# Attention and soft mixture of experts on one core: new TensorE order, V asked for two iterations before its cast, and on-chip homes for all experts' weights

## The chip, the cores and the metric

The kernel runs on one core of a Trainium2 chip. The metric is the device time of one execution in microseconds (us), as the median of several executions. Most numbers about stages come from one profiled execution of each kernel, whose span is 1.5 to 2 us shorter than the time of the same run. The profiled run of the kernel before took 241.13 us, 3.2 us above its median, so differences between its profile and the others may be too large by about that much. A run is called fast when it is within 1.5% of the fastest run of the same kernel, and slow otherwise.

## The reference

Eight batches of eight heads attend causally over 576 tokens and 16 beacon keys. The result, 4608 tokens of 512 values, goes through a soft mixture of eight experts.

```python
scores = scale * np.matmul(q, k_all.transpose(0, 1, 3, 2))   # q, k, v: (8, 8, 576, 64); 16 beacon keys ahead
a = softmax(causal(scores));  x = a @ v_all                   # x: (4608, 512)
logits = x @ phi                                              # 32 slots
slot_input = softmax_over_tokens(logits).T @ x                # (8 experts, 4 slots, 512)
slot_out[e] = np.maximum(slot_input[e] @ w1[e], 0.0) @ w2[e]  # w1: (8, 512, 1024), w2: (8, 1024, 512)
return softmax_over_slots(logits) @ slot_out
```

All inputs are float32: Q and K 18.9 MB, V 9.4 MB, weights 33.55 MB. The output is 9.44 MB. The experts can only start after attention, because `slot_input` needs every token; their weights can come at any time for which there is room.

## The kernel before

Attention runs in 32 iterations, one for each pair of heads. In an iteration the pair's scores are made in four steps (`score`, TensorE, then exp on ScalarE and causal masks on GpSimd), the previous pair is multiplied by V (`attend`), and the next pair's Q and K are transposed (`transp`, TensorE, copied out of PSUM by VectorE). Once in four iterations a batch is complete and its routing pieces (transposes, logits, slot sums) are mixed in.

V of the next batch is requested by SyncE and cast to float16 by GpSimd (even chunks) and VectorE (odd chunks). The weights are requested by GpSimd in pieces of 1 MiB, and the transfer casts them to float16: its queue wrote 16.78 MB for 33.55 MB of float32.

```python
    qkp = ctx.enter_context(tc.tile_pool(name="qkp", bufs=5))     # Q and K pairs
    vfp = ctx.enter_context(tc.tile_pool(name="vfp", bufs=6))     # V chunks
    wh = ctx.enter_context(tc.tile_pool(name="wh", bufs=6))       # weights of six experts
    # ... cut ...
    beacons()
    transp(0)
    for n in range(NP + 1):
        b, g = divmod(n, H // 2)
        # ... cut: flags for the last turn
            score(n, 0)
            for _ in range((0, 2, 3, 2)[n % 4]):
                if work:
                    work.pop(0)()          # routing pieces of the batch before
            score(n, 1)
            transp(n + 1)                  # ends with the copy of the beacon keys on GpSimd
            attend(n - 1, 0)
            score(n, 2)
            attend(n - 1, 1)
            score(n, 3)
            load_pair(n + 5)
            load_v(b + 1, g)               # V chunks 0 and 1, 2, 3, 4 for g = 0, 1, 2, 3
            for c in ((), (0, 1), (2,), (3, 4))[g]:
                cast_v(b + 1, c)           # chunk 4: requested and cast in the same iteration
            if n % 3 != 2 and n >= 3 and wl < 24:
                load_w(wl)                 # one piece of 1 MiB in two of three iterations
                wl += 1
    # ... cut: slot inputs
    layer1(0)
    for e in range(E):
        turn(e)
        if e + 1 < E:
            widen(e + 1)                   # experts 6 and 7 into the buffers of experts 0 and 1
            layer1(e + 1)
        layer2(e)
    # ... cut: output stage
```

The softmax here doesn't subtract the row's maximum and nothing guards it: scores larger than these inputs give would overflow.

## Time and profile before

| | before |
|---|---|
| time, median of 4 runs | 237.95 us (237.39 to 240.46) |
| span of the profiled run (241.13 us) | 239.2 us |
| attention, first to last mask | 12.2 to 171.0 us |
| first matmul of the experts | 181.9 us |
| end of the experts | 210.6 us |
| TensorE busy, share of the span | 74% |
| VectorE, ScalarE, GpSimd | 56%, 56%, 37% |

No engine is busy more than three quarters of the time, so the engines' shares alone name no limit. The prediction below shows how the slices, the list of waits, GpSimd's order of work and the table of stretches are read for it.

### The profile page before, as it was taken

How to read it: one execution, taken by the hardware profiler on the slowest of the kernel's cores; microseconds unless marked ns; L12 is line 12 of the kernel's file. 1: busy time of each engine (PE TensorE's matmuls, PEld its weight loads, DVE VectorE, ACT ScalarE, POOL GpSimd, SP SyncE). 2: the span in 40 equal slices, each digit the busy share in tenths (PEclk: the TensorE clock that was granted, in tenths of full speed). 3: DMA queues.
4: the chain of work that ended last, by engine and by line, in shares of the span. 5: the costliest groups of instructions: out<-in, count | busy, mean ns of one | idle time of the engine just before them, and what ended most of it. 6: DMA issues, size and time to landing. Idle time of an engine off the chain costs nothing.

```text
span 239.2 us, 7827 instructions
## 1 busy us (share of the span) xinstructions
PE 176.9 (74%) x3384; PEld 122.3 (51%) x3384; DVE 134.3 (56%) x315; ACT 133.8 (56%) x195; POOL 88.7 (37%) x165
## 2 busy tenths in 40 slices
PE   0689577987986898997798879799867874578400
PEld 0567455765675776765566666676654221123100
DVE  1591873675777467876576847566654231159600
ACT  2176473677777387886767738487721342149500
POOL 2091625354552644634636165434552700000000
PEclk9999795899999599999979979899995578559955
DMA  6999999999999998999999989564689999919995
GB/s 210 220 328 229 257 256 235 268 201 250 303 271 240 204 258 247 216 285 247 237 307 267 242 180 266 81 95 84 91 137 206 209 206 210 177 77 417 414 425 249
DMA packets 63714, 55.62 MB, mean 233 GB/s; under 512 B 41920, under 2 KB 50112, under 8 KB 62656
## 3 DMA queue, kind: packets, MB, share of 16 engines
q1 hardware_dynamic: 50880, 38.35, 56.9%
q0 software_dynamic: 12800, 16.78, 41.5%
q8 instruction: 26, 0.43, 0.8%
q14 instruction: 8, 0.07, 0.1%
HBM read 62.46 MB, written 9.44 MB: 301 GB/s over the span
## 4 chain that ended last, share of the span: by engine, by line
PE 33%; DMA 27%; ACT 13%; POOL 7%; DVE 5%; SPq 5%; issue 3%; DVEq 0%; ACTq 0%; POOLq 0%
DMA vf<-in_v_dram 17%; ACT ex L209 10%; DMA w2h<-in_moe_w_dram 8%; PE sc L203 8%; PE av L230 6%; PE tr L188 5%; PE tr L257 4%; PE fp L448 3%; SPq L103 2%; ACT osb L450 2%; POOL ex L211 2%; DVE xT L262 2%; PE tr L272 2%; SPq L88 2%; DMA kf<-in_k_dram 2%
## 5 line engine op out<-in xcount | busy, mean ns | idle before, releaser
L209 ACT ACTIVATE ex<-sc 128x1024 f16<-128x1024 f32 (+3 forms) x128 | 107.0, 869 | 59.8 <-PE sc L203 59.5
L203 PE MATMUL sc<-qT,kT 64*128 64x128 bf16 (+5 forms) x576 | 49.8, 269 | 18.5 <-POOL kT L193 8.7
L211 POOL TENSOR_SCALAR_AFFINE_SELECT ex<-ex 128x1024 f16<-128x1024 f16 x32 | 35.0, 1093 | 44.7 <-ACT ex L209 44.6
L230 PE MATMUL av<-vh,ex 128*128 128x65 f16 (+2 forms) x960 | 47.7, 206 | 0.7 <-issue 0.5
L230 PEld LDWEIGHTS <-ex 128*128 128x128 f16 (+2 forms) x960 | 40.2, 113 | 10.2 <-issue 8.3
L203 PEld LDWEIGHTS <-kT 64*128 64x128 bf16 (+1 forms) x576 | 21.7, 106 | 30.1 <-issue 15.3
L190 DVE COPY qT<-tr 128x576 bf16<-128x576 bf16 x32 | 24.2, 757 | 21.3 <-PE tr L188 21.3
L238 DVE TENSOR_TENSOR xb<-av,r 128x320 f16<-128x320 f32 x64 | 31.5, 491 | 2.2
L244 POOL CAST vh<-vf 128x512 f16<-128x512 f32 (+1 forms) x24 | 15.0, 629 | 28.0 <-DMA vf<-in_v_dram 28.0
L190 DVE COPY kT<-tr 128x576 bf16<-128x576 bf16 x32 | 23.9, 748 | 1.0 <-PE tr L188 0.9
L262 DVE COPY xT<-tr 128x1024 f16<-128x1024 f16 x16 | 10.7, 688 | 15.4 <-PE tr L257 15.4
L188 PE MATMUL tr<-idb,kf 64*64 64x64 bf16 x576 | 17.1, 206 | 2.2 <-issue 1.4
L188 PE MATMUL tr<-idb,qf 64*64 64x64 bf16 x576 | 17.1, 208 | 0.0
L188 PEld LDWEIGHTS <-qf 64*64 64x64 bf16 x576 | 13.5, 120 | 6.8 <-issue 6.4
L409 DVE CAST hs<-sc 128x512 f16<-128x512 f32 x8 | 5.5, 691 | 19.2 <-ACT hs L408 19.2
L188 PEld LDWEIGHTS <-kf 64*64 64x64 bf16 x576 | 14.8, 121 | 3.0 <-issue 2.8
L257 PE MATMUL tr<-idh,xb 128*128 128x128 f16 (+1 forms) x160 | 14.2, 247 | 2.3 <-issue 1.2
L217 POOL TENSOR_SCALAR_AFFINE_SELECT ex<-ex 80x160 f16<-80x160 f16 x32 | 10.6, 331 | 13.4 <-ACT ex L209 13.3
L237 DVE RECIPROCAL r<-av 128x5 f32<-128x5 f32 x64 | 12.0, 187 | 5.8 <-PE av L230 5.3
L450 ACT ACTIVATE osb<-fp,rc 128x512 f32<-128x512 f32 x18 | 11.8, 686 | 4.9 <-PE fp L448 4.4
L120 POOL DMA_DIRECT2D w1h<-in_moe_w_dram x16 | 11.5, 724 | 6.7 <-PE sc L404 6.7
L452 DVE TENSOR_SCALAR osb<-fp,rc 128x512 f32<-128x512 f32 x18 | 12.6, 747 | 1.4 <-PE fp L448 1.1
(58 smaller groups left out, 151.1 us busy)
## 6 DMA issues: line engine op xcount, KB each, us to landing
qf<-in_q_dram SPq DMA_DIRECT2D x32, 288.0 KB, 6.2
kf<-in_k_dram SPq DMA_DIRECT2D x32, 288.0 KB, 6.4
w1h<-in_moe_w_dram POOLq DMA_DIRECT2D x16, 512.0 KB, 8.7
w2h<-in_moe_w_dram POOLq DMA_DIRECT2D x16, 512.0 KB, 8.8
out_dram<-osb SPq DMA_DIRECT2D x8, 1024.0 KB, 8.8
vf<-in_v_dram SPq DMA_DIRECT2D x24, 256.0 KB, 7.5
vf<-in_v_dram SPq DMA_DIRECT2D x8, 224.0 KB, 7.2
vf<-in_v_dram SPq DMA_DIRECT2D x8, 160.0 KB, 7.5
```

The lines of the kernel that those rows point to most:

```text
L188: nc.tensor.transpose(tp[po:po + 64, j, :], hi, idb[po:po + 64, po:po + 64])
L190: nc.vector.tensor_copy(out=dst[:, Nb:Nb + S].rearrange("p (s j) -> p s j", j=J), in_=tp[:, :, :].rearrange("p j s -> p s j"))
L203: nc.tensor.matmul(sc[0:kn, a, col:col + un], kT[n % 3][64 * a:64 * a + 64, P * c:P * c + kn], qT[n % 3][64 * a:64 * a + 64, u0:u0 + un], ...
L209: nc.scalar.activation(ex[n][:, :, o:o + w], sc[:, :, 0:w], AF.Exp, scale=scale)
L211: nc.gpsimd.affine_select(out=ex[n][:, :, 0:512].rearrange("p a (c t) -> p a c t", c=4), in_=ex[n][:, :, 0:512].rearrange("p a (c t) -> p ...
L230: nc.tensor.matmul(avs[a][0:m, i * DD:(i + 1) * DD], ex[n][0:kn, a, o:o + m], vh[b % 2][0:kn, c, h, :], start=(c == 0), stop=(c == i))
L238: nc.vector.tensor_tensor(out=xb[b % 2][:, :, h, :], in0=avv[:, :, 0:D], in1=r5[:, :].unsqueeze(2).broadcast_to([P, NCH, D]), op=AL.mult)
L244: (nc.vector if c % 2 else nc.gpsimd).tensor_copy(out=vh[b % 2][0:kn, c, :, 0:D], in_=vf[(b, c)][0:kn])
L257: nc.tensor.transpose(tp[:, ii, t, 0:m], xb[b % 2][0:m, i, 2 * t:2 * t + 2, :].rearrange("p h d -> p (h d)"), idh[0:m, 0:m])
L262: nc.vector.tensor_copy(out=xT[b][:, :, P * cs[0]:P * cs[0] + 2 * P].rearrange("p t (i u) -> p i t u", i=2), in_=tp[:, :, :, :])
L450: nc.scalar.activation(osb[:, j, :], fp_[:, :], AF.Copy, scale=rc[:, i:i + 1])
L452: nc.vector.tensor_scalar(out=osb[:, j, :], in0=fp_[:, :], scalar1=rc[:, i:i + 1], scalar2=None, op0=AL.mult)
```

## The change

The intent is a steady TensorE: transposes two pairs ahead at the end of each iteration, one routing piece at a time, V cast two iterations after its request, and room on chip for the weights of all eight experts, by using the Q, K and V buffers again once they have been read. The weights are asked for at a set pace, faster from iteration 26.

```diff
-    qkp = ctx.enter_context(tc.tile_pool(name="qkp", bufs=5))
-    vfp = ctx.enter_context(tc.tile_pool(name="vfp", bufs=6))
-    wh = ctx.enter_context(tc.tile_pool(name="wh", bufs=6))
+    NQK, NVF, NWB = 5, 6, 6
+    qs = [const.tile([P, J, D], FP, name=f"qs{i}") for i in range(NQK)]
+    # ... ks, vs, wa, wb likewise
+    homes = [wt[:, 1024 * i:1024 * (i + 1)] for e in range(NWB) for wt in (wa[e], wb[e])
+             for i in range(4)]
+    # ... experts 6 and 7: float16 views of qs, ks in the order in which they come free, then vs
+    def pace(n):                           # in half MiB of float32 weights
+        if n < 26:
+            return 2 * max(0, (n - 2) * 16 // 23)
+        return 32 + 4 * (n - 25)
     for n in range(NP + 1):
+            if n + 2 < NP:
+                beacon_keys(n + 2)
             score(n, 0)
-            for _ in range((0, 2, 3, 2)[n % 4]):
-                if work:
-                    work.pop(0)()
             score(n, 1)
-            transp(n + 1)
+        route()                            # one routing piece
             attend(n - 1, 0)
             score(n, 2)
             attend(n - 1, 1)
+        route()
             score(n, 3)
-                load_pair(n + 5)
-                load_v(b + 1, g)
-                for c in ((), (0, 1), (2,), (3, 4))[g]:
-                    cast_v(b + 1, c)
-                load_w(wl)
+            transp(n + 2)
+            load_pair(n + 2 + NQK)
+        for m in ((0, 1) if n == 0 else (n + 1,)):
+            # ... load_v of part m (batch m // 4 + 1)
+        # ... cast_v of part n - 1: requested two iterations before
+        weights(pace(n))
```

## The prediction

> **What bounds the kernel now.** I read the page's forty slices first, then the list of waits, then GpSimd's order of work around one of those waits, and last a table of stretches for what the transfers do. In the slices the last two rows are the transfer engines' busy share and rate, the first the granted TensorE clock.
>
> ```profile
> PEclk9999795899999599999979979899995578559955
> DMA  6999999999999998999999989564689999919995
> GB/s 210 220 328 229 257 256 235 268 201 250 303 271 240 204 258 247 216 285 247 237 307 267 242 180 266 81 95 84 91 137 206 209 206 210 177 77 417 414 425 249
> ```
>
> A slice is 6 us. Transfers are busy everywhere except slices 25 to 28 (150 to 174 us, the last six or so of the 32 pair iterations), where they move 81 to 95 GB/s, and slice 35 (210 to 216 us). Yet slices 30 to 34 (180 to 210 us) are again full, and they are the experts' weights, which could have moved in the hole. That is one loss. The other is in the waits, whose columns are total us, times, longest:
>
> ```profile
> ACT ex L209 <- PE sc L203: 59.5, 69, 9.1
> ...
> POOL vh L244 <- DMA vf<-in_v_dram: 28.0, 9, 5.0
> ...
> PE sc L203 <- POOL kT L193: 8.7, 4, 3.0
> ```
>
> GpSimd waits nine times, 28.0 us in all, to cast a V chunk. It takes its instructions in order, so what stands behind that cast is late too:
>
> ```profile
> 71.73 0.20 POOL L193 COPY kT<-bkT 128x16 bf16<-128x16 bf16 x1
> 76.29 0.61 POOL L244 CAST vh<-vf 80x512 f16<-80x512 f32 x1 [4.37 <-DMA vf<-in_v_dram]
> 76.86 1.09 POOL L211 TENSOR_SCALAR_AFFINE_SELECT ex<-ex 128x1024 f16<-128x1024 f16 x1
> ```
>
> The columns are start, duration, instruction, and idle time before it. The 80-row chunk is asked for and cast in the same iteration (g = 3), so 4.37 us of transfer time are waited out; the mask of the next pair comes 0.6 us after it. That mask marks each iteration; its 32 instances run from 12.2 us to 171.0 us:
>
> ```profile
> L211 POOL TENSOR_SCALAR_AFFINE_SELECT ex<-ex x32: 1085/1091/1112, 12.2 to 171.0; 128x1024 f16<-128x1024 f16 x32
> ```
>
> (171.0 - 12.2) / 31 = 5.12 us an iteration, while the two last, with no V wait, take 4.78 and 4.80 (161.46, 166.24, 171.04). TensorE is busy 134.4 us of that stretch at a mean clock of 0.91, so about 122 / 31 = 3.9 us an iteration at full clock (an estimate; it takes all busy time to scale with the clock). ScalarE is busy 108.6 us, 3.5 an iteration. Neither engine alone accounts for 5.12.
>
> The transfers are nearer to it than they look. In the table of stretches the last two columns are the transfer share (over 1 when two packets overlap) and the GB/s written on chip:
>
> ```profile
> 8.50:12.50 4.00, 2.69 (x68) 2.27 (x68) 2.06 (x4) 1.36 (x2) 0.46 (x2) 1.00 1.36 207
> 14.50:17.50 3.00, 3.00 (x65) 2.43 (x59) 3.00 (x8) 1.93 (x3) 2.80 (x7) 1.00 1.07 393
> 96.00:122.00 26.00, 22.50 (x517) 17.11 (x512) 18.59 (x43) 18.61 (x26) 13.39 (x25) 0.94 1.15 251
> ...
> 150.00:174.00 24.00, 21.16 (x467) 16.14 (x465) 15.36 (x40) 17.43 (x24) 11.27 (x20) 0.93 0.52 83
> ...
> 194.00:200.00 6.00, 4.32 (x64) 1.53 (x57) 2.08 (x3) 2.46 (x5) 0.00 (x0) 0.99 1.21 209
> ...
> 219.00:231.00 12.00, 4.70 (x17) 1.59 (x14) 6.38 (x10) 5.67 (x9) 0.00 (x0) 0.88 1.01 419
> ```
>
> The first row is V alone: 207 GB/s. The second is Q and K alone: 393. The fifth is weights alone: 209 GB/s of float16 written, so 418 of float32 read. The last is the output: 419. From the sizes in the reference: V with its beacons 9.7 MB / 207 = 46.9 us; Q and K 18.9 MB / 393 = 48.0; weights 33.55 MB / 418 = 80.3; small inputs 1; so 176 us of input, and output 9.44 MB / 419 = 22.5. In all 199 of 239 us. The times add when the queues share the engines: from 96 to 122 us the packet counts (6990 under 512 B, so V; 1102 of Q and K; 2.08 MB of weights written) make 8.7 + 6.5 + 10.0 = 25.1 us of such work in 26 us, 96%. So the input transfers are a floor close under everything else.
>
> [...]V goes in 256 B pieces and the trace has it at 207 GB/s against 393 for Q and K in 2304 B pieces[...]the 78 to 84 us slice, after the wait shown, has a clock of 0.5.[...]
>
> **The change, part by part.**
> 1. V is asked for one iteration earlier and cast one later, two iterations apart (about 9 us; the median V landing is 7.1 us, the longest 10.2). All but the very first casts should find their data. Removed: most of the 28.0 us of GpSimd wait[...]. The first batch's request still has one iteration's lag, so one wait near 24 us stays.
> 2. Beacon keys are copied two iterations ahead at the head of GpSimd's work: the 8.7 us of score matmuls waiting for kT go. Transposes two pairs ahead at the end of an iteration take their copies off the path to the next score; the routing pieces come one per slot instead of two or three together. The instruction counts on TensorE don't change (6,770 rows in both).
> 3. By iteration 25 both kernels have asked for 16 MiB of weights. After that the old one asks for 4 MiB to iteration 31, then 4, and the last 8 only from 183 us, when the buffers of experts 0 and 1 are read. The new one asks for 12 MiB in the same six iterations and the last 4 directly after, into used Q, K and V buffers. Its cost: up to four issues of 0.72 to 0.76 us on GpSimd in iterations 30 and 31, beside 1.4 us of masks: 4.3 us, just an iteration. The hole of 24 us at 83 GB/s written (166 read, 40% of 418) fills: 14 us.
>
> Sum, on the old trace's clock:
> - First mask at 12.2 us, unchanged.
> - To iteration 25: Q and K 0.59 MB / 393 = 1.50, V 0.303 MB / 207 = 1.46, weights 16.8 MB in 23 iterations, 0.73 MB / 418 = 1.75; 4.7 us of transfer, 4.9 at 96%. Some 8 us may be behind at the end (a weight piece or two in flight, V's two iterations), so I take 4.6 us: above the 4.2 to 4.4 that I estimate for TensorE with few gaps. 25 x 4.6 = 115.
> - Six more at 4.4, with TensorE the limit: 26.4. The last mask is at 153.6, against 171.0.
> - From the last mask to the first expert matmul: 10.8 us (171.04 to 181.86), unchanged. So 164.4.
> - Experts: the first five took 181.86 to 195.47, 2.72 each, mostly at half clock; 8 x 2.72 and 1 for the end make 22.8. So 187.2 if all weights are there.
> - Weights all landed: 2.5 + 176 / 0.95 = 188. The last half expert is used within 1 us: 189. The two limits nearly meet; I take 189, against 210.6 in the old trace.
> - From there to the end 28.6 us (210.6 to 239.2), of which 22.5 are the output. Span 217.6; the old span is 1.5 above the median time, so 216 us.
>
> The gain of about 21 us is not the sum of what is removed (28 of GpSimd waits, 8.7 of kT, 14 of hole, and these expert stalls):
>
> ```profile
> 202.39 0.61 PE L404 MATMUL sc<-w1h,siT 128*32 128x512 f16 x2 [2.37 <-DMA w1h<-in_moe_w_dram]
> ...
> 204.94 1.04 PE L404 MATMUL sc<-w1h,siT 128*32 128x512 f16 x6 [1.94 <-DMA w1h<-in_moe_w_dram]
> ```
>
> They overlap, and the transfers' floor stops all of them.
>
> **Rivals.** (a) Transfers stay at 96% or better and the hole goes completely: last weight at 183, experts at full clock, 211 us. For it: stretches of the old trace reach it. Against: start-up, and the expert stage ran at half clock. (b) The faster attention makes the queues collide: V, in small packets beside more weights, comes later than two iterations, the casts wait again, only later, and transfers run at 90%: last weight at 198, about 225 us. For it: landings up to 10.2 us, near the 9.2 us lag. Against: the lookahead of Q and K grows too, and a late weight costs attention nothing. (c) GpSimd or VectorE becomes the bound: four weight issues and the masks in the last iterations, or VectorE's 105 us in the 159 us stretch packed into 141. It would add 3 to 5 us, 220. (d) All weights on chip but nothing gained, because only the order of the same bytes moves: excluded by the hole, which is real idle time.
>
> **Range and chances.** 216.5 us, 210 to 224 from (a) and most of (b). Over 2% faster needs below 232.9; even (b) gives that. Faster 0.96, same 0.03, slower 0.01.
>
> **What would show it.** Last mask near 154 us; GpSimd's wait for V under 8 us, mostly near 24 us; no score wait for kT; no hole before the last mask, transfers full to about 188; the experts with little or no wait for weights; clock 0.9 or more in attention; the output stage unchanged. It is wrong if iterations stay near 5 us with V waits (b), if TensorE alone holds them at 4.8, or if experts 6 and 7 still wait several us for weights.

## The result, and the profile after

The changed kernel takes 228.97 us (median of 4 runs, 227.28 to 230.84) beside 237.95 for the kernel before. The ratio is 0.958, with a 95% interval of 0.947 to 0.969. A ratio here is the mean time of one kernel's fast runs over that of the other's of the same rounds, so it is not quite the ratio of the medians. The kernel is faster, as forecast, but by 9 us and not by 21, and 229 lies outside the range of 210 to 224.

| | before | predicted | after |
|---|---|---|---|
| last mask (us) | 171.0 | 153.6 | 166.6 |
| first matmul of the experts | 181.9 | 164.4 | 177.1 |
| last weight landed | about 210 | 188 | between 193 and 194 |
| end of the experts | 210.6 | 189 | 198.1 |
| span | 239.2 | 217.6 | 226.5 |

The slices of the changed kernel, in the same rows as before (clock, transfer share, GB/s; a slice is now 5.7 us):

```profile
PEclk9999859997999699859997999997999679959955
DMA  6999989999999999999999999969999999139996
GB/s 202 243 295 381 204 236 258 246 286 215 261 312 216 239 207 246 239 214 227 310 250 264 297 225 241 260 107 208 193 209 209 208 207 205 33 158 416 418 422 255
```

The hole of four slices at 81 to 95 GB/s is gone. One slice with a 6 (slice 26, 147 to 153 us, 107 GB/s) is what remains of it, and from slice 27 to 33 the weights' plain stream runs at 193 to 209 GB/s. So the part of the change that was to fill the hole did so.

The waits (total us, times, longest) are where the surprise is:

```profile
POOL vh L270 <- DMA vs<-in_v_dram: 35.6, 13, 7.8
...
DVE vh L270 <- DMA vs<-in_v_dram: 13.2, 4, 6.3
```

GpSimd waited 28.0 us for V before and waits 35.6 now. VectorE waited 4.6 for V and waits 13.2. Together that is 48.8 us where the prediction had "under 8 us" for GpSimd. The waits of score matmuls for GpSimd's copies into kT are gone from the list, as forecast (one of 0.9 us for VectorE's copy stays, as before). The masks run to 166.6 us:

```profile
L237 POOL TENSOR_SCALAR_AFFINE_SELECT ex<-ex x32: 1090/1094/1139, 12.2 to 166.6; 128x1024 f16<-128x1024 f16 x32
```

The mean iteration is (166.6 - 12.2) / 31 = 4.98 us, only a little under the 5.12 of before, although many iterations without a wait now take 4.1. Two masks are 10.4 us apart around 90 to 100 us. First, from SyncE's order of work, a request for V (start, duration, what is asked for), then, from GpSimd's, a cast and the mask behind it (the last column is the idle time before, and what ended it):

```profile
80.92 0.39 SPq L100 DMA_DIRECT2D vs<-in_v_dram  x1
```

```profile
99.40 0.61 POOL L270 CAST vh<-vs 80x512 f16<-80x512 f32 x1 [7.84 <-DMA vs<-in_v_dram]
...
100.58 1.09 POOL L237 TENSOR_SCALAR_AFFINE_SELECT ex<-ex 128x1024 f16<-128x1024 f16 x1 [0.43 <-ACT ex L235]
```

The V chunk asked for at 80.92 us is cast by VectorE at 95.94, 15.0 us later, and GpSimd waits 7.84 us for another chunk, with the mask of the next pair behind it. Beside it were three pieces of weights, asked for by GpSimd at 79.94, 83.84 and 87.40 us in the view of GpSimd's order. At the solo rates of the prediction, three pieces are 3.15 MB / 418 = 7.5 us. SyncE's requests from 74.84 to 80.92 us, four of Q and K and two of V, are 3.0 and 2.5 us. That is an estimate of 13.0 us for what was in front of the chunk or beside it.

The experts run from their first matmul to the end without a wait for weights, in 21.1 us:

```profile
177.05 1.04 PE L449 MATMUL sc<-wa,siT 128*32 128x512 f16 x8
...
198.13 0.75 DVE L477 TENSOR_SCALAR soh<-av,rd 128x512 f16<-128x512 f32 x1 [1.91 <-PE av L467]
```

Before they took 28.8, with 5.4 us of waits for weights in the trace. The output stage takes 28.4 us (28.6 before).

### The profile page after: what moved, and what is told of

The parts are those of the page before. It is cut to its first block, busy times and chain, and to the rows that moved or that the text cites.

```text
span 226.5 us, 7849 instructions
## 1 busy us (share of the span) xinstructions
PE 167.2 (74%) x3384; PEld 118.3 (52%) x3384; DVE 136.5 (60%) x315; ACT 131.0 (58%) x195; POOL 93.2 (41%) x173
## 4 chain that ended last, share of the span: by engine, by line
PE 30%; DMA 26%; ACT 15%; DVE 11%; SPq 6%; issue 4%; POOL 2%; DVEq 0%; ACTq 0%; POOLq 0%
DMA vs<-in_v_dram 22%; ACT ex L235 10%; PE sc L229 7%; PE av L256 7%; PE tr L212 5%; DMA qs<-in_q_dram 3%; PE sc L449 3%; SPq L100 3%; DVE hs L454 2%; PE fp L489 2%; SPq L89 2%; PE tr L283 2%; ACT hs L453 2%; DVE xT L288 2%; DVE xb L264 2%
## 5 line engine op out<-in xcount | busy, mean ns | idle before, releaser
L237 POOL TENSOR_SCALAR_AFFINE_SELECT ex<-ex 128x1024 f16<-128x1024 f16 x32 | 35.1, 1096 | 39.3 <-ACT ex L235 39.3
L229 PE MATMUL sc<-qT,kT 64*128 64x128 bf16 (+5 forms) x576 | 44.6, 263 | 4.3 <-ACT ex L235 2.0
L270 POOL CAST vh<-vs 128x512 f16<-128x512 f32 (+1 forms) x24 | 14.8, 620 | 35.6 <-DMA vs<-in_v_dram 35.6
L229 PEld LDWEIGHTS <-kT 64*128 64x128 bf16 (+1 forms) x576 | 21.2, 103 | 12.5 <-issue 7.2
L263 DVE RECIPROCAL r<-av 128x5 f32<-128x5 f32 x64 | 12.3, 192 | 22.3 <-PE av L256 21.9
L214 DVE COPY kT<-tr 128x576 bf16<-128x576 bf16 x32 | 23.9, 748 | 2.5 <-PE tr L212 2.4
L212 PE MATMUL tr<-idb,ks 64*64 64x64 bf16 x576 | 16.7, 202 | 7.2 <-issue 2.7
L212 PEld LDWEIGHTS <-ks 64*64 64x64 bf16 x576 | 15.5, 116 | 9.3 <-issue 8.7
L212 PE MATMUL tr<-idb,qs 64*64 64x64 bf16 x576 | 16.9, 204 | 2.0 <-DMA qs<-in_q_dram 1.8
L270 DVE CAST vh<-vs 128x512 f16<-128x512 f32 x16 | 10.1, 638 | 13.2 <-DMA vs<-in_v_dram 13.2
L212 PEld LDWEIGHTS <-qs 64*64 64x64 bf16 x576 | 13.0, 117 | 6.2 <-DMA qs<-in_q_dram 2.0
L489 PE MATMUL fp<-soh,eLh 128*128 128x512 f16 x36 | 12.3, 456 | 2.0 <-DVE soh L477 0.8
L302 PE MATMUL tr<-xT,phih 128*128 128x288 f16 x64 | 12.7, 287 | 0.6 <-DVE xT L288 0.3
L283 PEld LDWEIGHTS <-xb 128*128 128x128 f16 (+1 forms) x160 | 10.4, 108 | 3.8 <-issue 3.3
```

Of the source, the lines that this page charges most:

```text
L212: nc.tensor.transpose(tp[po:po + 64, j, :], hi, idb[po:po + 64, po:po + 64])
L214: nc.vector.tensor_copy(out=dst[:, Nb:Nb + S].rearrange("p (s j) -> p s j", j=J), in_=tp[:, :, :].rearrange("p j s -> p s j"))
L229: nc.tensor.matmul(sc[0:kn, a, col:col + un], kT[n % 3][64 * a:64 * a + 64, P * c:P * c + kn], qT[n % 3][64 * a:64 * a + 64, u0:u0 + un], ...
L237: nc.gpsimd.affine_select(out=ex[n][:, :, 0:512].rearrange("p a (c t) -> p a c t", c=4), in_=ex[n][:, :, 0:512].rearrange("p a (c t) -> p ...
L270: (nc.vector if c % 2 else nc.gpsimd).tensor_copy(out=vh[b % 2][0:kn, c, :, 0:D], in_=vs[(NCH * b + c) % NVF][0:kn])
L283: nc.tensor.transpose(tp[:, ii, t, 0:m], xb[b % 2][0:m, i, 2 * t:2 * t + 2, :].rearrange("p h d -> p (h d)"), idh[0:m, 0:m])
```

## The experiments

Theory A: the transfer engines are full, the weights compete there with V, and the waits for V are the symptom. Theory B: V is late because it stands behind Q and K in SyncE's queue with too short a notice. Ratios are to the kernel before in the same rounds. The kernel before and the changed kernel differ by one to two per cent from one set of rounds to the next (the changed kernel had 0.958, 0.968 and 0.952), so kernels are best compared within a set. The waits differ more: the changed kernel's three profiles have 48.8, 67.3 (`after_again`) and 60.5 us (`after_third`, a slow run) of waits for V on GpSimd and VectorE together, and last masks at 166.6, 164.8 and 169.4. Where a profile fell in a slow run this is said, and it is used for waits only.

### First set: what do the weights do to V?

**e2_no_weights.** All weights after attention, in one look.

```diff
     def pace(n):
-        if n < 26: ...
+        return 0
```

> No weights at all are asked for during attention; all 32 MiB come after it. Theory A: the waits for V fall under 12 us in all (mostly the one near 21 to 28 us), iterations take 4.1 to 4.4 us, last mask at 142 to 150. Theory B: the waits stay above 30 us and the last mask after 158. Either way the whole is slower, about 250 us, since 80 us of weights follow attention.

```profile
POOL vh L270 <- DMA vs<-in_v_dram: 7.1, 1, 7.1
...
DVE vh L270 <- DMA vs<-in_v_dram: 5.2, 1, 5.2
```

```profile
L237 POOL TENSOR_SCALAR_AFFINE_SELECT ex<-ex x32: 1090/1096/1098, 12.6 to 145.5; 128x1024 f16<-128x1024 f16 x32
```

Two waits remain, both at the start (before the mask at 26.8 us), and the iterations take 3.99 to 4.38 us from iteration 7 to 30, 4.15 in the mean. The last mask comes at 145.5 us. The whole takes 263.6 us (250 forecast), since 80 us of weights follow. The landings of V, from request to data, in the changed kernel and then here:

```profile
DMA to landing us min/median/max: 3.6/6.8/15.0
```

```profile
DMA to landing us min/median/max: 3.3/4.5/6.6
```

So V's notice is enough without weights beside it, but only just. It isn't the 8.3 us that two iterations would be. Of batches 2 to 6, one chunk is asked for by SyncE and cast by GpSimd at

```profile
70.35 0.38 SPq L100 DMA_DIRECT2D vs<-in_v_dram  x1
```

```profile
77.02 0.61 POOL L270 CAST vh<-vs 128x512 f16<-128x512 f32 x1
```

which is 6.7 us apart, and over all 25 chunks of these batches it is 5.0 to 8.5 us, 6.8 in the mean; each landed at least 0.5 us before its cast. With the weights beside it, half of all landings take 6.8 us or more, and the longest 15.0. (e2 also frees GpSimd of the weights' requests, 0.72 to 0.76 us each; but the landings shorten too, and they don't wait for GpSimd.) The stretch from 30 to 140 us of this run shows what is left for weights (TensorE busy first, clock, transfer share and GB/s last):

```profile
30.00:140.00 110.00, 102.78 (x2555) 80.89 (x2554) 91.38 (x220) 89.54 (x130) 50.53 (x99) 0.98 0.74 193
```

TensorE is busy 102.8 of 110 us here, so 4.15 us is close to the bound of TensorE in this order. Q, K and V need 2.96 us of transfers in each iteration (1.50 + 1.46), which leaves 1.19 us, or 0.50 MB of weights. The change asks for 0.73 MB, 1.75 us. By this estimate it asks for more than fits, and someone must wait. Theory A's forecast is met (the waits are 12.3 us where it had "under 12"), theory B's is not.

**e1_slow_pace.** 12 MiB instead of 16 before iteration 26.

```diff
-            return 2 * max(0, (n - 2) * 16 // 23)
-        return 32 + 4 * (n - 25)
+            return 2 * max(0, (n - 2) * 12 // 23)
+        return 24 + 4 * (n - 25)
```

> Weights asked for more slowly up to iteration 25 (12 MiB in place of 16), the rest later. Theory A (the transfer engines are full, and the weights take their share away from V, so the waits for V are its symptom): GpSimd and VectorE wait for V under 30 us in place of 49, the last mask comes 4 to 8 us earlier than 166.6, but the last weight lands at 190 to 194 as before, so experts 6 and 7 now wait and the whole gains 1 to 4 us. Theory B (V is late because it stands behind Q and K in SyncE's queue and its two iterations are too short a notice): waits for V within 10% of 49 us, last mask within 2 us of 166.6, time within 1%.

The median is 226.19 us, ratio 0.951 (0.942 to 0.961). The waits for V are 17.3 and 3.9 us, the last mask comes at 159.8, 6.8 us earlier, and the experts end at 196.1, only 2 us earlier, because the experts' stage now takes 25.8 us in place of 21.1, with 2.5 us of waits for weights and a mean clock of 0.64 in place of 0.82. Each number is as theory A had it, but the longer stage is only partly a wait for weights. Against the changed kernel the gain is within the noise between sets.

**e3_v_first.** V ahead of Q and K in each iteration.

```diff
-        if n + 2 + NQK < NP:
-            load_pair(n + 2 + NQK)
         for m in ((0, 1) if n == 0 else (n + 1,)):
             ... load_v
+        if n + 2 + NQK < NP:
+            load_pair(n + 2 + NQK)
```

> In each iteration V is asked for before the Q and K pair instead of after it. Theory A: the order in one queue moves about 1.5 us of transfers, waits for V fall by at most a third, time within 1.5% of the changed kernel. Theory B: waits for V fall by half or more (under 25 us), last mask at 158 or earlier, 4 us or more faster than the changed kernel.

The median is 224.80 us, ratio 0.944 (0.935 to 0.953). No run of the changed kernel is in this set; against its 0.952 to 0.968 in others this is 1 to 2.5% faster, about the noise between sets. The waits for V in its profile (a slow run) were 51.3 and 17.1 us. That is no less than in the changed kernel's three profiles, so theory B's forecast of half the waits is refuted, and theory A's of up to a third less isn't met either. Order in the queue by itself doesn't take the waits away.

**e4_v_wide.** V's bytes as rows of 2 KB, wrong (the values land in the wrong places).

```diff
-        nc.sync.dma_start(out=t[p0:p0 + hi - lo], in_=v[b, :, lo:hi, :].rearrange("h p d -> p h d"))
+        nc.sync.dma_start(out=t[p0:p0 + hi - lo].rearrange("p h d -> p (h d)"),
+                          in_=v[b].rearrange("h s d -> (h s d)").rearrange("(p f) -> p f", f=H * D)[lo:hi])
```

> Wrong result on purpose: the same number of V bytes, but read as contiguous rows of 2 KB per partition in place of 256 B pieces, so V should move at nearly 393 GB/s instead of 207: 24 us of transfer work in place of 47. Theory A: waits for V fall under 15 us, last mask at 145 to 155, and the whole is 15 to 22 us faster than the changed kernel (some 207 to 214 us). Theory B, in which the notice and not the amount of transfer counts: it gains too, but less than 8 us.

The median is 218.36 us, ratio 0.915 (0.903 to 0.926): about 10 us faster than the changed kernel (which wasn't in this set), between the two forecasts. The waits were 15.9 and 4.9 us. The last mask came at 156.3 and the experts ended at 188.4 us. The amount of transfer work matters, but 23 us less of it (an estimate, at Q and K's rate) gave less than half of that. What held attention then was not tested; its iterations 7 to 25 still took 4.70 us in the mean, where e2 has 4.14.

### Second set: the parts alone

**e6_before_no_weights.** The kernel before without weights in attention (its three lines around `load_w(wl)` in the loop removed), one look.

> The kernel before, with no weights asked for during attention (they follow, as far as its buffers allow). Told apart from the changed kernel without weights (4.15 us an iteration, one pair of waits for V near 20 us, last mask 145.5), it shows what the order alone is worth when nothing competes. If order and notice matter by themselves: the 80-row chunk, asked for and cast in the same iteration, still makes GpSimd wait in most batches, 10 to 25 us in all, undisturbed iterations stay at 4.7 to 4.8, last mask at 162 to 170. If only the competition of the weights mattered: waits for V under 8 us and last mask under 155.

GpSimd waits 10.3 us for V and VectorE 3.9. That lies in the range of the first forecast by its number only: all but 0.3 us of it comes before 33 us, and not in most batches. The last mask comes at 154.4 us, which fits the second. I had misread the old kernel: its iterations of 4.7 to 4.8 us are followed by one of 3.4 in each batch, so that its undisturbed mean is 4.43 us and not 4.78. Without competition, then, the new order is worth 154.4 - 145.5 = 9 us. With the weights in attention the two orders end only 4.4 us apart (171.0 and 166.6). The notice of V tells what the new loop lost: without weights, the old one has 6.3 to 11.4 us between request and cast for the first four chunks of a batch and 5.0 to 5.4 for the fifth (batches 2 to 6), the new one 5.0 to 8.5 and 6.0 to 6.5. In the program the new notice is an iteration longer. But V stands behind Q and K in SyncE's queue, and these use again the buffers that the new loop's last transposes read in the same iteration, the old loop's in the one before. In the changed kernel's trace SyncE waits 28.1 us in all, in 14 waits, for transposes before it can ask for Q or K; what such waits cost in e2 was not shown.

**e7_homes_only.** The loop of the kernel before, with the new homes and pace.

```diff
-    (loop of the changed kernel)
+    (loop of the kernel before: transp(n + 1), routing in twos and threes, V cast as before;
+     ends with weights(pace(n)))
```

> The old order of the loop with the new homes and the new pace of the weights: the third part of the change alone. Theory A (transfers full, weights compete with V): the last mask does not come earlier than before, 170 to 176; no weights wait at the end; the first matmul of the experts after 181, their end near 204 to 206, and the whole 233 to 236, 1 to 2% faster than before. If the hole were worth its 14 us by itself, it would be 225 or less.

The median is 231.45 us, ratio 0.984 (0.969 to 1.000). The last mask is at 168.9 and the experts end near 200.9 us, somewhat better than forecast. The 14 us of the hole are worth some 4 us by themselves, in an interval that reaches 0.

**e8_order_only** was to be the reverse, the new order with the old weights.

```diff
-    homes += spare
+    homes += homes[0:16]                   # experts 6 and 7 where 0 and 1 were
-        if n < 26: ...                     # pace as in the kernel before
+        return 2 * len([i for i in range(3, n + 1) if i % 3 != 2])
+            weights(8 * (e + 1 + NWB))     # ahead of layer1(e + 1)
```

> The new order, V timing and key copies, with the old weights: 20 MiB during attention, 4 after it, the last 8 into the buffers of experts 0 and 1 when those have been read. Theory A: last mask at 160 to 166, and the experts wait for weights as in the kernel before, ending 28 to 29 us after their first matmul, so 229 to 233 us, 2.5 to 4% faster than before. If the V timing were worth nothing while weights compete: last mask after 168, within 1.5% of before.

It gave a wrong result and 245.61 us: I had put the request for expert 6 ahead of the second layer of expert 0 in program order, so that this layer read expert 6's weights. It tells nothing. **e8b_order_only** puts the request after `layer2(e)`.

> e8 mended: the weights of experts 6 and 7 are asked for after the second layer of experts 0 and 1 has been issued, so they overwrite nothing that is still read. New order and V timing, old weights. Theory A: last mask at 160 to 166 (e8 had 164.4), the experts end 26 to 29 us after their first matmul because the last 8 MiB are asked for only then; 229 to 234 us. With the weights alone at 0.984 of before and the whole change at 0.958, additive parts would give 0.974 here. If the V timing were worth nothing while weights compete: 0.985 or more.

> The changed kernel as it is, once more, to stand beside the others of this call on one chip: 226 to 231 us, 0.95 to 0.965 of before; last mask 163 to 170, waits for V 40 to 70 us.

Both were in one set. e8b has ratio 0.968 (0.957 to 0.979) and the changed kernel 0.968 (0.959 to 0.978). With the old weights the last mask comes at 160.1 us and the first expert matmul at 170.6, but the experts wait and end at 199.0. With the new homes (the profile of that set) the last mask comes at 164.8, the first expert matmul at 175.3, and the experts end at 198.3. So in this set filling the hole gained nothing that can be seen: attention ended 4.7 us later, and the experts' stage (28.4 us without the homes, 23.0 with them) was about as much shorter. The weights of the last iterations explain only a part of the 4.7 us. At iteration 25, where both kernels have asked for 16 MiB, e8b, whose first piece is asked for an iteration sooner, is already 3.2 us ahead (134.7 and 137.8); the six iterations after that take 25.4 and 27.0 us. Whether the parts add isn't settled: e8b's interval holds the 0.974 of its forecast, and 0.968 times e7's 0.984 is 0.953, beside 0.952 to 0.968 for the whole.

### Third set: a better pace and more notice

**c3_deep_slow_vfirst.** Nine V buffers, three iterations of notice, V first, and a slow pace (14 MiB by iteration 28).

```diff
-    NQK, NVF, NWB = 5, 6, 6
+    NQK, NVF, NWB = 5, 9, 6
-        for m in ((0, 1) if n == 0 else (n + 1,)):
+        for m in ((0, 1, 2) if n == 0 else (n + 2,)):   # and ahead of load_pair
-        if n < 26: ...
+        if n < 29:
+            return 2 * max(0, (n - 2) * 14 // 26)
+        return 28 + 4 * (n - 28)
```

> Weights slowed to 12 to 14 MiB up to iteration 28, nine V buffers with V asked for three iterations before its cast, and V ahead of Q and K in the queue. Theory A: waits for V under 20 us, last mask at 148 to 155; the total of transfers is unchanged, so the last weight cannot land before 186 to 190 and the experts wait for it; 217 to 222 us, faster than the changed kernel by 3 to 5%. If transfers are not what limits the whole, the last weight lands before 183 and the time is under 214.

The median is 230.15 us, ratio 0.974 (0.959 to 0.990). The waits for V fell to 8 us as forecast and the last mask came at 156.2 (148 to 155 forecast), but the last weight landed near 199 (186 to 190), and the time was missed by 8 us. The row of GB/s in the slices of c3 shows why (a slice is 5.7 us):

```profile
GB/s 195 240 308 325 211 242 218 286 243 217 325 232 250 298 254 247 292 203 243 320 255 218 313 245 29 115 158 193 203 211 206 209 207 207 131 136 411 426 418 257
```

In slices 24 to 26 (138 to 155 us) the rate is 29, 115 and 158 GB/s: all Q, K and V had been requested and the weights not yet. The old hole had opened again. Attention gained 10 us and the experts, which waited 8 us for weights in all, gave it back.

**c5_ramp11** and **c6_ramp8** were to close it, with 11 and 8 MiB before iteration 24 and three pieces an iteration from there.

```diff
+        if n < 24:
+            return 2 * max(0, (n - 2) * 11 // 21)          # c6: 8
+        return min(48, 22 + 6 * (n - 23)) + 4 * max(0, n - 28)   # c6: 16
```

> As c3 (nine V buffers, three iterations of notice, V ahead of Q and K), but the weights speed up at iteration 24, when the last Q, K and V are asked for, so that the hole of c3 at 130 to 150 us doesn't open; 11 MiB before that. Theory A: last mask 152 to 158, last weight at 180 to 187 and not 198, the whole 216 to 221 us, 4% faster than the changed kernel. If the hole was not what cost c3 its gain: 226 or more.

> As c5 with 8 MiB before iteration 24. Theory A: transfers of Q, K, V and weights then just fit under 4.2 us an iteration, last mask 147 to 153, last weight still 180 to 187 because the total is the same, the experts wait a little for the last weights; 213 to 219 us, the same as c5 or up to 2% faster. If the pace before iteration 24 doesn't matter: last mask as in c5 within 2 us.

Both missed by far: 234.19 us (three of its four runs slow) and 238.34, ratio 0.996 (0.982 to 1.011). The hole did close: no slice is under 157 GB/s until the last weights. In c5 the last V chunks landed up to 23.9 us after their request and GpSimd waited 8.2 and 11.9 us for two of them. In c6 the waits for V were 10.5 us, and its pace (0.40 MB or 0.96 us an iteration before iteration 24) is less than the 1.19 us that e2 leaves. Yet its iterations 7 to 25 took 4.68 us in the mean, with three of 5.3 to 7.1 us between 97 and 116 us, in which TensorE's transposes waited (for what, the trace doesn't say). After that, GpSimd's own requests waited (both profiles are of slow runs):

```profile
163.66 0.53 POOL L138 DMA_DIRECT2D qs<-in_moe_w_dram  x1 [2.00 <-DMA wb<-in_moe_w_dram]
166.22 0.53 POOL L138 DMA_DIRECT2D ks<-in_moe_w_dram  x1 [2.03 <-DMA wb<-in_moe_w_dram]
166.75 1.11 POOL L237 TENSOR_SCALAR_AFFINE_SELECT ex<-ex 128x1024 f16<-128x1024 f16 x1
```

The brackets of the first two lines say that each request for weights waited 2 us until an earlier piece had landed, and the mask at 166.75 us stands behind them. The trace's semaphores show what the wait is: GpSimd's 40 transfers use eight of them in turn, and a request waits until the transfer eight before it has landed. The one at 163.66 us starts 0.3 us after the landing of the piece asked for at 142.39. In the changed kernel's trace the last eleven requests, from 169.50 us on, each start 0.28 to 0.53 us after such a landing. In c6 GpSimd's requests waited 23.5 us in all for earlier pieces, and the masks with them: those at 154.50, 166.75 and 177.00 us are 12.3 and 10.3 us apart.

### Fourth set: one piece at a time

Four kernels in one set of five rounds, with the changed kernel among them. **f1_notice_only** has nine V buffers and three iterations of notice, all else as in the change. **f2_steady_ramp** adds V first and the pace `2 * max(0, (n - 2) * 13 // 23)` up to iteration 25, then `26 + 4 * (n - 25)`. **f3_early_start** is f2 with

```diff
+        if n < 26:
+            return 2 * (n * 14 // 25)
+        return 28 + 4 * (n - 25)
```

> The changed kernel with nine V buffers and V asked for three iterations before its cast in place of two; order in the queue and pace of the weights as they are. If the short notice is what my prediction missed: waits for V 15 to 25 us in place of 49 to 67, last mask 156 to 161, and the whole 1 to 2.5% faster than the changed kernel of this call. If the share that the weights take is what counts and more notice only lengthens the queue: waits for V above 35 us, within 1%.

> Nine V buffers, V ahead of Q and K, 13 MiB of weights before iteration 26 in place of 16, then two pieces of 1 MiB an iteration as in the change. If both V's notice and a weight pace that fits beside 4.2 us iterations are needed: waits for V 10 to 25 us, last mask 153 to 159, last weight 187 to 191 because the transfers' total is what it was, the whole 2 to 3.5% faster than the changed kernel of this call (221 to 225 us). If the last weight is at 195 or later, a hole opened again, as in c3.

> As f2, but the weights start at iteration 2 in place of 4 and reach 14 MiB before iteration 26, so that the stretch from 20 to 40 us, which carried only 83 to 89% of its transfers, is filled. Last weight 2 to 4 us earlier than in f2 (184 to 188) if that stretch was idle for want of requests; the waits for V near 25 us grow by 1 to 3 us; the whole 0 to 1% faster than f2.

> The changed kernel, to stand beside the others of this call: 226 to 231 us.

| | median us | ratio to before | 95% interval |
|---|---|---|---|
| after_third (the change) | 230.39 | 0.952 | 0.945 to 0.959 |
| f1_notice_only | 225.01 | 0.934 | 0.928 to 0.940 |
| f2_steady_ramp | 223.55 | 0.924 | 0.918 to 0.930 |
| f3_early_start | 220.36 | 0.919 | 0.915 to 0.923 |

f1 gains 0.934 / 0.952, 1.8%, with waits for V of 43 us (60.5 in `after_third`; both are slow runs): its times fit one forecast and its waits the other. f2's gain is in its forecast, and in its profile (a slow run) the waits are 13.5 us and the last mask comes at 158.6, but the last weight landed near 192 and not by 191. f3 is 3.4% faster than the change (0.919 / 0.952). Its waits and its masks:

```profile
POOL vh L270 <- DMA vs<-in_v_dram: 6.1, 2, 5.0
...
DVE vh L270 <- DMA vs<-in_v_dram: 4.5, 1, 4.5
```

```profile
L237 POOL TENSOR_SCALAR_AFFINE_SELECT ex<-ex x32: 1084/1090/1197, 12.5 to 157.1; 128x1024 f16<-128x1024 f16 x32
```

10.6 us of waits, last mask at 157.1, experts from 167.6 to 189.1 us, and the span is 217.5. The share of the transfers carried from 20 to 40 us, counted from packets at the solo rates, rose from about 84% in the changed kernel to 96%, and the last weight landed near 186 us, as forecast.

**g1_pace_only** is the changed kernel with the pace of f3 and nothing else, beside **f3_again**, in a last set.

> The changed kernel with the pace of f3 alone (weights from iteration 2, 14 MiB before iteration 26), V with six buffers, two iterations of notice and behind Q and K as in the change. If pace and notice are both needed: waits for V 25 to 45 us, last mask 160 to 166, 224 to 228 us. If the pace was all: waits for V under 15 us and 219 to 222 us, like f3. If the notice was all: 228 to 231 us, like the changed kernel.

> f3 once more, to stand beside g1 on one chip: 219 to 223 us, last mask 155 to 159.

g1 takes 223.17 us, ratio 0.940 (0.928 to 0.952); f3 again 222.85, ratio 0.938 (0.927 to 0.949). They can't be told apart in time. Yet g1's waits for V are:

```profile
POOL vh L270 <- DMA vs<-in_v_dram: 38.3, 17, 6.4
...
DVE vh L270 <- DMA vs<-in_v_dram: 9.1, 6, 5.3
```

47.4 us, as in the change, but in 23 waits of at most 6.4 us, where the changed kernel had 17 of up to 7.8. The last mask is at 160.7 us, against 157 and 161.4 in f3's two profiles (the second is outside its forecast). No forecast of g1 fits whole: mask and waits are nearest to the first, and the time falls between the first two. So the sum of the waits for V is no measure of the time. One reason can be read in the same profiles: GpSimd's idle time before casts and masks together is 74.9 us in the change (35.6 for V, 39.3 for exp), 70.1 in g1 (38.3, 31.8) and 67.6 in f3 (6.1, 61.5). Most of the time in which f3 doesn't wait for V it waits for exp. That a short wait costs little is suggested by this, not shown. The pace alone gives most of what f3 gives. How much the longer notice adds to it stays open within these intervals.

f3 is the fastest correct kernel, and is faster than both the kernel before and the changed one.

## Why the prediction was wrong

The direction was right, and parts 2 and 3 of the mechanism did what they should: the waits for kT went and the hole filled. Part 1 failed, and with it the second term of the sum: "Some 8 us may be behind at the end, so I take 4.6 us". I had worked out 4.9 us of transfers an iteration and then credited 8 us of them to lookahead. The profile has iteration 25 at 137.5 us: (137.5 - 12.2) / 25 = 5.01 us, so 125.3 us in place of 115, more than even 4.9 would give. No such credit is to be seen. Weights that are behind don't lie idle; they share the engines with V, and V is what the next iterations wait for. This rests on e2, where the same loop without weights has 4.15 us an iteration and waits for V only at the start. Part 1's "all but the very first casts should find their data" fell with it: GpSimd waited 35.6 us for V, not under 8.

Part 1 also had its notice wrong. "Two iterations apart (about 9 us)" is 5.0 to 8.5 us even without weights (e2), less than the old loop gave four of five chunks (e6), while half of the change's landings take 6.8 us or more. How much of the 10.3 us each of the two errors cost isn't separated: f1, with one iteration more notice and the same pace, gains 1.8% in its set, and g1, with another pace and the same notice, 1 to 3% against the change in other sets.

By its other steps:

- First mask 12.2 us: measured 12.2.
- Six more iterations at 4.4: 29.1 us in place of 26.4. One wait of 6.15 us for the last batch's V lies in them.
- Last mask to the first expert matmul, 10.8: measured 10.5.
- Experts 22.8: measured 21.1. The first three take 2.67 to 2.78 us each (granted clock 0.60 from 177.05 to 185.2 us) and the later ones 2.24 (0.96 from there to 198.1), so this was too high.
- All weights by 188 us: 193 to 194. 176 us of transfers in 191 us is 92%, not 95%. In the change this wasn't the limit, as its experts didn't wait for weights; in e1 they waited 2.5 us and in c3 8.
- Experts' end to the end of the span, 28.6: measured 28.4.
- The half clock of the old 78 to 84 us slice: TensorE had been idle for 1.8 us (76.2 to 78.0) when the clock fell to 0.5. What lowers it was not shown.
- "The two last, with no V wait, take 4.78 and 4.80" was read rightly but is not the old loop's undisturbed mean, which is 4.43 (e6).

The end of the experts is thus later than the 187.2 of the engines' path by 10.3 + 2.7 - 0.3 - 1.7 = 11.0, with 0.1 lost in rounding: 198.1.

Of the rivals, (b) came closest. It named later V beside more weights, the wait moved and not removed, and landings beyond the lag (15.0 us measured). But it put the damage into the transfers' efficiency, and what bound was the end of attention. I argued against (b) that a late weight costs attention nothing. It was the wrong question: an early weight costs attention its V.

f3's first profile, of the fastest of its six runs, comes near the predicted path: last mask 157.1 (predicted 153.6), first expert matmul 167.6 (164.4), end of the experts 189.1 (189), span 217.5 (217.6). Its second profile is 3 to 4 us later at each point (161.4, 171.9, 193.0, 220.9). That the ends agree so well is partly luck, for f3 differs from the change in pace, notice and order of requests, and its pace too, 1.40 us an iteration, is more than the 1.19 us that e2 leaves; its first 25 iterations took 4.68 us each. I had the change's transfers at 4.9 us an iteration, above TensorE's 4.2 to 4.4, and passed over what follows from it: that V would be what waits.

## What to carry to other kernels

Before a transfer that can wait is moved beside one that can't, subtract what the urgent stream needs in an iteration at the compute-bound pace; by the estimate (2.96 of 4.15 us in e2, so 1.19 us are left) only about that rest can be asked for without someone waiting (c6 kept within it and still lost, so it isn't enough). The request should start as soon as there is idle transfer time and not be saved up for a burst: here f3 and g1, which start early, had ratios of 0.919 and 0.940, and c6 with its burst 0.996. Measure a notice from request to cast in a trace; the program's count of iterations isn't it. A hole in the transfers and the waits elsewhere may be one budget seen twice, so don't count on the sum of their gains. Read a wait beside the idle time that its engine has in any case, and not by its sum alone.

## What the transfers and their requests showed

- The 256 B pieces of V landed at most 6.6 us after the request with no weights beside them (e2), 15.0 us with the change's pace of weights, and 23.9 us in c5 (a slow run).
- Alone, 256 B pieces ran at 207 GB/s and 2304 B pieces at 393 (8.5 to 12.5 and 14.5 to 17.5 us of the kernel before), 1.9 times the time for a byte.
- In c6 requests from GpSimd waited up to 2.8 us each for an earlier piece, because this program's transfers share eight semaphores. SyncE's requests have eight of their own (124 requests in the changed kernel's trace). In the changed kernel its waits that ended with an input's landing are some 5 us in all, and what they cost V was not tested.
